# Later loads, one more addition on VectorE and later subtractions in a fused dynamic convolution and maxout layer

## The chip, the cores and the metric

The kernel runs on one core of a Trainium2 chip. The metric is the device time of one execution in microseconds (us), lower is better. Engines are named as the profile names them: PE is TensorE (PEld its weight loads), DVE is VectorE, ACT is ScalarE, POOL is GpSimd, SP is SyncE, which here only starts transfers.

## What is computed

The reference takes x (8 batches of 4160 positions with 192 channels), softmax logits weight_gen (8 heads, 7 taps per position) and three weight matrices. Cut to what matters:

```python
w = softmax(weight_gen, axis=-1)                       # 7 taps for each of 8 heads
x_pad = concatenate([zeros((B, 6, D)), x], axis=1)
out[b, s, h, g] = sum_k w[b, s, h, k] * x_pad[b, s + k, h, g]
x2 = out.reshape(33280, 192)
h1 = x2 @ w1 ; h2 = x2 @ w2                            # 192 x 1024 each
result = maximum(h1, h2) @ w_out                       # 1024 x 192
```

So each position is a weighted sum of itself and the six positions before it, followed by a two-branch layer with a maximum and an output product. The kernel uses max(h1, h2) = h1 + relu(h2 - h1): PE multiplies y by the difference w2 - w1 (the tile `wd`), ACT takes the relu, and the part y @ w1 @ w_out goes through a product `w10` of 192 x 192.

## The kernel before, in words

**Layout.** Partition p holds 260 consecutive positions of one batch element, called columns. `BATCHES` cuts the 260 columns into 16 groups of 16 and one of 4, `UNITS` cuts these into 8 units of 4 columns (batches 0 and 1 of the schedule) and after them units of 8. A unit of n columns gives n `TILES`, each a share of the 1024 hidden features for all columns of the unit. The order of the columns is rotated by 8: what the schedule calls column c of batch 0 is column c + 8 of a partition (`actual`, line 106).

**Stages of one unit.** The exponential of the logits (`exp_sum`, line 158, ACT), the sums over taps (`red`, 178, DVE), their logarithm (`ln`, 182, ACT), its subtraction from the logits (`shift`, 188, DVE), the exponential of the result as bf16 weights (`weights`, 194, ACT), the product of the weights with seven shifted views of x (`mul`, 208, and for the very first units `mul_pair`, 224, DVE), and the sum of the seven products. From batch 2 on that sum is three additions on DVE (`adds`, 234) into `y_t`, and a DMA transposes it (`transpose`, 258), behind which a small cast on POOL (`gate`, 270) waits and releases the next loads. In batches 0 and 1 PE forms sum and transpose together: `sum_part` (296) multiplies the products by an identity, tap by tap, for three of six blocks at a time, and ACT copies the result into `yt` (316). Where `adds` is called with `first=True`, DVE adds taps 3 to 5 to taps 0 to 2, and PE sums only the taps of `LEFT` = (0, 1, 2, 6). Before, this is done for unit 5.

**Hidden and output.** `hid_tile` (354) computes a tile of h2 - h1 in PSUM, `relu` (369) copies it to `rd_t` on ACT, and the output columns are accumulated in PSUM from `rd_t` (`out_hidden`, 394) and from y (`out_first`, 409), copied by ACT (`evac`, 470) and stored by SP.

**What sets the order.** Each engine executes its instructions in program order, which the kernel writes by hand. `hidden(g)` (552) emits one group of two or three tiles together with the output columns that are due, and calls back at set places: `amid` ahead of the group's last hidden tile, `between` after the copies, `beside` for the stages of later batches (ahead of the last relu where four columns go out, at the end where two do). `early` (905) lists what the first groups do there. From tile 16 on, `extra` (956) emits DVE's work for later batches at fixed tiles, `adds` takes a `beside` that puts pieces of `shift` or `red` between its additions, and ACT's exponentials and logarithms are given a due tile in `due` (929), with exceptions in `AT` and with a rule in `softmax_steps` that puts a long one off.

**Start.** SP issues the first logits, the first ten columns of x (`xs`, cast by DVE into `xb_t`), and the weight matrices; POOL issues the rest of x as casting loads, each held behind an instruction by `behind` (325). The load of schedule columns 4 to 7 of batch 0 (columns 12 to 15 of a partition) is `load_x(0, 4, 4)`. `mul_pair(0, 4, 0, 0, 4)` (line 714) multiplies taps 0 to 3 of its first two columns and needs none of it, `mul_pair(0, 4, 0, 4, K)` (719) is the first to need it. `w_diff` (686) forms the parts of `wd` on DVE, `halves_swapped` (690) swaps their halves through PE and ACT. `keep_warm` (667) runs matmuls whose result is not used. `wrap_mask` (148) zeroes, on ACT, the halo of the unit in which the rotated columns wrap around, ahead of the product for the second half of batch 15.

Of the kernel before, what the change touches and what calls it, by code (L numbers as in the profile page):

```python
# [23 lines left out]
def kernel(  # L24
# [27 lines left out]
    NB = len(BATCHES)  # L52
# [105 lines left out]
    def exp_sum(b, i=0, of=1):  # L158
        if i == 0:
            e_ts[b] = pe_.tile([P, BATCHES[b][1] * WGC], FP32, name="e_t", tag="e")  # L160
        w = BATCHES[b][1] * WGC // of
        return nc.scalar.activation(out=e_ts[b][:, i * w:(i + 1) * w], in_=wg_ts[b][:, i * w:(i + 1) * w], func=AF.Exp)  # L162
# [120 lines left out]
    LEFT = (0, 1, 2, K - 1)  # L283
# [332 lines left out]
    with tc.tile_pool(name="pstage", bufs=1) as pstage:  # L616
# [40 lines left out]
        nc.vector.tensor_single_scalar(out=msk_i, in_=msk_i, scalar=RPB - 1, op=ALU.bitwise_and)  # L657
        nc.vector.tensor_single_scalar(out=msk_i, in_=msk_i, scalar=1, op=ALU.min)
        nc.vector.tensor_copy(out=msk, in_=msk_i)
        first_exp = exp_sum(0, 0, 2)  # L660
        for step in (red, ln, shift):
            step(0, 0, 2)
        weights(0, 0)
# [13 lines left out]
        for j, parts in enumerate((((0, PAD), (PAD, 2)), ((PAD + 2, 2),))):  # L677
            for at, n in parts:
                nc.vector.tensor_copy(out=xb_ts[0][:, at * D:(at + n) * D], in_=xs[:, at * D:(at + n) * D])
            first_mul = mul_pair(0, 0, j)  # L680
            if j == 0:
                keep_warm(8, True)
        w1 = {kind: pstage.tile([P, w], BF16, name="w1" + kind)
              for kind, w in (("E", F), ("T", HF))}
# [13 lines left out]
        w1t = pstage.tile([P, F + HF], BF16, name="w1t")  # L698

        w_diff("E", 0, 0)  # L700
        behind(first_exp, load_x(0, 4, 4))
        behind(first_mul, load_x(0, 8, 4))
        load_x(0, 12, 4)
        for h in range(2):
# [8 lines left out]
            nc.sync.dma_start_transpose(out=w1t[:, c0:c0 + w].rearrange("p (b t) -> p b t", t=P), in_=w1[kind])  # L713
        mul_pair(0, 4, 0, 0, 4)
        sum_transpose(0, amid=lambda: halves_swapped(0, warm[:, 512:1024]))
        keep_warm(2)
        w_diff("T", 0, 2)
        halves_swapped(2, warm[:, 0:512])
        mul_pair(0, 4, 0, 4, K)
# [93 lines left out]
    def end_of_1():  # L813
        mul(1, 12)
        shift(2)


    def sums_in_range():
# [76 lines left out]
    none = lambda: None  # L895
    begun = {}

    def first_of_sum(u):
        begun[u] = sum_part(u, 0, 3)

    def rest_of_sum(u):
        sum_part(u, 3, 6)
        begun[u]()

    early = {
        3: (none, rest_of_1),
        4: (lambda: (behind(relu_of[8], load_x(2, 0, 8, halo=False)),
                     rest_of_sum(4), behind(yt_of[4], load_wg(4, nc.gpsimd)), ln(2)), end_of_1),
        5: (lambda: (exp_sum(3), red(3), sum_transpose(5, LEFT), weights(2, 0)), none),
        6: (lambda: (weights(2, 8), ln(3), rest_of_sum(6)), none),  # L910
        7: (lambda: (behind(relu_of[14], load_x(2, 8, 8)), rest_of_sum(7)), none),
    }
# [13 lines left out]
        ('l', 12, 0): 162,  # L926
        ('l', 5, 0): 45,
    }
    due = {}
    for c in range(3, NB):  # L930
        soon = c < 8
# [24 lines left out]
    def extra(t):  # L956

        u, k = TILES[t]
        b, o, n = UNITS[u]
        s = o + k  # L960

        if s == 0 and b + 1 < NB:
            mul(b + 1, 0)
        later = 0 if b < 4 else 5
        if s == later and b + 1 < NB:

            c = b + 1
            adds(c, 0, beside=lambda i, of: shift(c + 1, i, of) if c + 1 < NB else None)
        if s == 8 and b == NB - 3:
            wrap_mask()  # L970
        if s == 8 and b + 2 < NB:
            mul(b + 1, 8)
        if s == 8 + later and b + 2 < NB:
            adds(b + 1, 8, beside=lambda i, of: red(b + 3, i, 2) if b + 3 < NB and i < 2 else None)
        if k == n // 4 - 1 and 7 < u + 1 < NU:
            transpose(u + 1)

# [11 lines left out]
    for g in range(4, len(GROUPS)):  # L989
        if GROUPS[g][1] == 3 and "c" not in ps:  # L990
            later_ps()
        tiles = [t for t in range(GROUPS[g][0], sum(GROUPS[g])) if t >= 16]
        if g == 9:
            behind(relu_of[16], load_x(3, 0, 8))
        if g in early:
            hidden(g, OUTS[g], early[g][0],
                   amid=lambda: first_of_sum(g) if g != 5 else None)
            early[g][1]()
            steps(g, tiles)
        else:  # L1000
            hidden(g, OUTS[g], beside=lambda: steps(g, tiles))
# [35 lines left out]
```

## Time and profile before

| | us |
|---|---|
| median of 3 runs | 411.01 |
| lowest, highest | 410.79, 412.25 |
| the profiled execution | 411.17 |
| its span, first to last instruction | 409.4 |
| PE busy in it | 398.0 |
| DVE busy | 377.2 |
| ACT busy | 353.8 |

How to read the rows: a row of the timeline is start, busy time, engine, line, operation, what is written from what, shape and count; in brackets stands the idle time of the engine ahead of it and what ended that. A row of stretches has the length, then busy time and count of PE, PEld, DVE, ACT and POOL, the granted clock of PE, the share of the DMA engines and GB/s. Line numbers are those of the kernel before.

### The profile page before, as it was taken

Reading aid. Unit: us, or ns where it says so; the run is one execution under the profiler, and the core shown is the slowest. Engines: PE = TensorE matmul, PEld = TensorE weight load, DVE = VectorE, ACT = ScalarE, POOL = GpSimd, SP = SyncE. Lnnn points to the kernel's source line nnn. Section 1 sums busy time; section 2 is a strip of 40 time slices with the busy share of each in tenths; the row PEclk is TensorE's granted clock in tenths of the full one; section 3 lists DMA queues with packets and bytes.
Section 4 is the critical chain, followed back from the end, with each engine's and each line's share of the span. In section 5 each row is a group of like instructions: output and inputs, shape, how many; then the busy total and the mean of one; then the engine's idle time right before and its main releaser. Section 6 shows DMA issues by size and latency. Waiting matters only on the chain.

```text
span 409.4 us, 16186 instructions
## 1 busy us (share of the span) xinstructions
PE 398.0 (97%) x7406; PEld 317.0 (77%) x7406; DVE 377.2 (92%) x230; ACT 353.8 (86%) x418; POOL 81.2 (20%) x108
## 2 busy tenths in 40 slices
PE   8799999999999999999999999999999999999995
PEld 3588899777777877777777777877787777777795
DVE  6999999999999999999999999999999999999400
ACT  3889899999899998898988999999999889898781
POOL 1411012212221202221221122222111223120000
PEclk9999999999999999999999999999999999999998
DMA  8997298876657665776765676587478558835323
GB/s 242 250 176 208 66 194 152 170 170 164 162 114 210 188 141 117 231 200 87 230 186 109 143 217 188 107 214 187 103 120 250 145 107 228 171 79 158 98 79 120
DMA packets 65110, 66.32 MB, mean 162 GB/s; under 512 B 49425, under 2 KB 54161, under 8 KB 65040
## 3 DMA queue, kind: packets, MB, share of 16 engines
q1 hardware_dynamic: 56064, 40.54, 36.9%
q0 software_dynamic: 8832, 24.63, 29.3%
q8 instruction: 58, 0.95, 0.9%
q10 hardware_dynamic: 144, 0.10, 0.1%
q14 instruction: 12, 0.10, 0.1%
HBM read 37.33 MB, written 25.56 MB: 154 GB/s over the span
## 4 chain that ended last, share of the span: by engine, by line
PE 89%; ACT 6%; DMA 1%; issue 1%; SPq 1%; DVE 0%; ACTq 0%
PE op_ps L402 40%; PE hd L362 38%; PE op_ps L415 7%; ACT rd_t L372 3%; PE hdp L362 2%; PE yps L307 2%; DMA ws1T<-in_moe_w_dram 1%; ACT yt L316 1%; ACT e_t L162 0%; ACT o_t L487 0%; SPq L642 0%; ACT en_t L202 0%; SPq L625 0%; ACT xb_t L150 0%; SPq L634 0%
## 5 line engine op out<-in xcount | busy, mean ns | idle before, releaser
L372 ACT ACTIVATE rd_t<-hd 128x1024 bf16<-128x1024 f32 (+1 forms) x206 | 234.5, 1187 | 26.2 <-PE hd L362 25.0
L402 PE MATMUL op_ps<-wo,rd_t 64*128 64x192 bf16 x4160 | 210.6, 243 | 0.4 <-issue 0.4
L402 PEld LDWEIGHTS <-rd_t 64*128 64x128 bf16 x4160 | 180.8, 94 | 16.0 <-issue 0.6
L362 PE MATMUL hd<-yt,wd 64*128 64x512 bf16 (+1 forms) x1584 | 187.3, 360 | 0.4 <-ACT rd_t L372 0.4
L218 DVE TENSOR_TENSOR m_t<-xb_t,en_t 128x10752 bf16<-128x10752 bf16 (+1 forms) x35 | 181.5, 5191 | 0.8 <-ACT en_t L202 0.5
L362 PEld LDWEIGHTS <-wd 64*128 64x128 bf16 x1776 | 93.9, 94 | 44.8 <-issue 3.6
L270 POOL CAST gate<-yt 128x1 f32<-128x1 bf16 x29 | 42.1, 1451 | 257.8 <-DMA yt<-y_t 257.8
L244 DVE TENSOR_TENSOR m_t<-m_t 128x4608 bf16<-128x4608 bf16 (+1 forms) x30 | 74.1, 2470 | 0.1
L487 ACT COPY o_t<-op_ps 128x384 f32<-128x384 f32 (+1 forms) x99 | 57.1, 587 | 12.4 <-PE op_ps L402 12.4
L415 PE MATMUL op_ps<-w,yt 64*128 64x192 bf16 x768 | 54.7, 243 | 0.1
L415 PEld LDWEIGHTS <-yt 64*128 64x128 bf16 x768 | 37.8, 94 | 16.3 <-issue 1.1
L250 DVE TENSOR_TENSOR m_t<-m_t 128x3072 bf16<-128x3072 bf16 (+1 forms) x29 | 50.0, 1723 | 0.1
L202 ACT ACTIVATE en_t<-wg_t 128x896 bf16<-128x896 f32 (+2 forms) x45 | 35.8, 819 | 0.7 <-DVE wg_t L191 0.7
L253 DVE TENSOR_TENSOR y_t<-m_t 128x1536 bf16<-128x1536 bf16 (+1 forms) x29 | 27.3, 941 | 0.5
L133 POOL DMA_DIRECT2D xb_t<-in_x_dram x34 | 18.3, 538 | 32.9 <-ACT rd_t L372 22.0
L191 DVE TENSOR_TENSOR wg_t<-wg_t,ln_t 128x280 f32<-128x280 f32 (+5 forms) x46 | 22.1, 480 | 0.4 <-ACT ln_t L186 0.3
L372 ACT ACTIVATE rd_t<-hdp 128x1024 bf16<-128x1024 f32 x16 | 16.3, 1032 | 2.8 <-PE hdp L362 2.8
L162 ACT ACTIVATE e_t<-wg_t 128x896 f32<-128x896 f32 (+2 forms) x18 | 16.2, 903 | 1.3 <-DMA wg_t<-in_weight_gen_dram 1.3
L180 DVE TENSOR_REDUCE s_rest<-e_t 128x64 f32<-128x448 f32 (+2 forms) x27 | 16.3, 602 | 0.8 <-ACT e_t L162 0.8
L362 PE MATMUL hdp<-yt,wd 64*128 64x256 bf16 x192 | 13.9, 270 | 2.1 <-ACT rd_t L372 1.5
L477 DVE COPY o_last<-op_ps 128x192 f32<-128x192 f32 x1 | 0.4, 358 | 16.5 <-ACT o_last L477 16.5
L307 PE MATMUL yps<-ident,m_t 64*128 64x64 bf16 x636 | 12.5, 190 | 1.7 <-issue 1.1
(53 smaller groups left out, 89.8 us busy)
## 6 DMA issues: line engine op xcount, KB each, us to landing
out_dram<-o_t SPq DMA_DIRECT2D x22, 768.0 KB, 5.2
xb_t<-in_x_dram POOLq DMA_DIRECT2D x30, 384.0 KB, 5.1
out_dram<-o_t SPq DMA_DIRECT2D x20, 384.0 KB, 3.2
wg_t<-in_weight_gen_dram POOLq DMA_DIRECT2D x13, 448.0 KB, 5.3
xb_t<-xb_t POOLq DMA_DIRECT2D x15, 288.0 KB, 5.6
xb_t<-in_x_dram POOLq DMA_DIRECT2D x4, 192.0 KB, 6.7
xs<-in_x_dram SPq DMA_DIRECT2D x1, 576.0 KB, 3.8
ws0E<-in_moe_w_dram SPq DMA_DIRECT2D x2, 256.0 KB, 5.8
```

What stands on the lines that cost most here:

```text
L191: nc.vector.tensor_tensor(out=w_t, in0=w_t, in1=_sub(s_ts[b], hs.start, [[1, hs.stop - hs.start], [0, K]]), op=ALU.subtract)
L202: nc.scalar.activation(out=_sub(en_ts[b], (o * WGC + j * N * K) * 2, [[2 * N, K], [2, N], [1, 2]]), in_=_sub(wg_ts[b], (o * H + j * N) * K ...
L218: return nc.vector.tensor_tensor(out=m_out, in0=x_in, in1=_sub(en_ts[b], o * WGC * 2, [[2, K * n * H], [0, G // 2], [1, 2]]), op=ALU.mult,)
L244: nc.vector.tensor_tensor(out=taps(0, 1, 3), in0=taps(0, 1, 3), in1=taps(3, 1, 3), op=ALU.add)
L250: nc.vector.tensor_tensor(out=taps(0, 2, 2), in0=taps(0, 2, 2), in1=taps(1, 5, 2), op=ALU.add)
L253: nc.vector.tensor_tensor(out=_sub(y_ts[b], o * D, [[64, 2], [P, 3 * w // 2], [1, 64]]), in0=taps(0, 1, 1), in1=taps(2, 1, 1), op=ALU.add,)
L270: nc.gpsimd.tensor_copy(out=gate, in_=yt[:, 0:1])
L362: nc.tensor.matmul(hid_out(t, f, j), lhsT=wd_at(j, s, f // 4, f % 4 * P, P), rhs=_sub(yt_ts[u][half(j), :], (s + j) % 3 * P, [[3 * P, w // ...
L372: relu_of[t0] = nc.scalar.activation(out=rd[:, k * 1024:(k + n) * 1024], in_=hd[:, at:at + n * 1024], func=AF.Relu)
L402: return nc.tensor.matmul(op_out(c), lhsT=rd[half(r), k * 1024 + at:k * 1024 + at + P], rhs=wo[half(r), f * D:(f + 1) * D], start=start, s ...
L415: nc.tensor.matmul(op_out(c + j), lhsT=yt_ts[u][half(j), (3 * i + (s + j) % 3) * P:(3 * i + (s + j) % 3 + 1) * P], rhs=w10[half(j), s * D: ...
L487: nc.scalar.copy(out=_sub(o, c % 24 * D, [[D, len(qs)], [h * D, 2], [1, D]]), in_=_sub(tile_, at + (qs[0] - p) * D, [[D, len(qs)], [512, 2 ...
```

## The change

Four edits.

1. `load_x(0, 4, 4)` waits for the first product of DVE (`mul_pair(0, 0, 0)`) instead of the first exponential of ACT. The two matmuls of `keep_warm(2)` after the first sum are gone.
2. Unit 7 (schedule columns 28 to 31) gets the addition of taps 3 to 5 on DVE, and PE sums the four taps of `LEFT` for it.
3. In group 5 the exponential of batch 3 is emitted ahead of the last hidden tile and its relu, and no longer after the group's copies.
4. For batches 13, 14 and 15 `shift` is no longer spread in three pieces over the additions of the unit two ahead of its product, but comes in two pieces around the additions of the unit after that; the `weights` of these batches are due later (tiles 16 (c - 1) and 16 (c - 1) + 5).

```diff
-        first_exp = exp_sum(0, 0, 2)
+        exp_sum(0, 0, 2)
...
             first_mul = mul_pair(0, 0, j)
             if j == 0:
+                behind(first_mul, load_x(0, 4, 4))
                 keep_warm(8, True)
...
-        behind(first_exp, load_x(0, 4, 4))
         behind(first_mul, load_x(0, 8, 4))
         load_x(0, 12, 4)
...
         sum_transpose(0, amid=lambda: halves_swapped(0, warm[:, 512:1024]))
-        keep_warm(2)
         w_diff("T", 0, 2)
...
     def end_of_1():
         mul(1, 12)
         shift(2)
+        adds(1, 12, True)
...
+    TAPS = {7: LEFT}
+
     def first_of_sum(u):
-        begun[u] = sum_part(u, 0, 3)
+        begun[u] = sum_part(u, 0, 3, TAPS.get(u, range(K)))
 
     def rest_of_sum(u):
-        sum_part(u, 3, 6)
+        sum_part(u, 3, 6, TAPS.get(u, range(K)))
...
-        5: (lambda: (exp_sum(3), red(3), sum_transpose(5, LEFT), weights(2, 0)), none),
+        5: (lambda: (red(3), sum_transpose(5, LEFT), weights(2, 0)), none),
...
+    LATE = (13, 14, 15)
+    for c in LATE:
+        AT['W', c, 0], AT['W', c, 8] = 16 * (c - 1), 16 * (c - 1) + 5
...
-            adds(c, 0, beside=lambda i, of: shift(c + 1, i, of) if c + 1 < NB else None)
+            adds(c, 0, beside=lambda i, of: shift(c + 1, i, of) if c + 1 < NB and c + 1 not in LATE else None)
...
-            adds(b + 1, 8, beside=lambda i, of: red(b + 3, i, 2) if b + 3 < NB and i < 2 else None)
+            adds(b + 1, 8, beside=lambda i, of: (shift(b + 2, 0, 2) if i == 0 and b + 2 in LATE else None,
+                                                 red(b + 3, i, 2) if b + 3 < NB and i < 2 else None))
+            if b + 2 in LATE:
+                shift(b + 2, 1, 2)
...
-                   amid=lambda: first_of_sum(g) if g != 5 else None)
+                   amid=lambda: first_of_sum(g) if g != 5 else exp_sum(3))
```

## The prediction

> **What bounds the kernel now.** I read the page first, then the busy time by stretches, then the timeline of those stretches in which an edit lies.
>
> ```profile
> PE 398.0 (97%) x7406; PEld 317.0 (77%) x7406; DVE 377.2 (92%) x230; ACT 353.8 (86%) x418; POOL 81.2 (20%) x108
> ```
> ```profile
> 12.70:24.00 11.30, 9.03 (x241) 7.31 (x241) 11.20 (x12) 10.42 (x19) 3.23 (x6) 1.00 1.29 221
> ...
> 50.00:360.00 310.00, 309.74 (x5443) 245.31 (x5440) 309.55 (x174) 282.32 (x318) 68.10 (x81) 1.00 0.70 166
> ```
>
> The columns of the stretches are length, then busy time of PE, PEld, DVE, ACT and POOL. From 50 to 360 us PE works 309.74 of 310.00 us, so there only fewer matmuls or a new hole in PE matter. DVE works 309.55 us of them too, but ahead of PE. From 12.7 to 24 us it is DVE that never rests (11.20 of 11.30) while PE does (9.03): there DVE and, behind it, ACT set the pace. So an edit before 24 us is judged by DVE, a later one by PE.
>
> **Part 1: columns 12 to 15 of x later, two warm-up matmuls gone.**
>
> ```profile
> 4.20 0.68 POOL L133 DMA_DIRECT2D xb_t<-in_x_dram  x1 [2.79 <-ACT e_t L162]
> ...
> 6.54 1.56 DVE L227 TENSOR_TENSOR m_t<-xb_t,en_t 128x2688 bf16<-128x2688 bf16 x1
> ...
> 8.47 1.56 DVE L227 TENSOR_TENSOR m_t<-xb_t,en_t 128x2688 bf16<-128x2688 bf16 x1
> ...
> 10.34 1.06 POOL L133 DMA_DIRECT2D xb_t<-in_x_dram  x2 [5.47 <-DVE m_t L227]
> ...
> 12.12 0.69 DVE L687 TENSOR_TENSOR wd<-ws1T,ws0T 128x512 bf16<-128x512 f32 x1 [0.62 <-DMA ws1T<-in_moe_w_dram]
> ...
> 12.73 2.22 DVE L227 TENSOR_TENSOR m_t<-xb_t,en_t 128x1152 bf16<-128x1152 bf16 x2
> ...
> 14.87 0.61 DVE L180 TENSOR_REDUCE s_first<-e_t 128x64 f32<-128x448 f32 x1
> ...
> 15.59 0.25 ACT L186 ACTIVATE ln_t<-s_first 128x64 f32<-128x64 f32 x1
> ```
>
> The load now waits for the first multiplication, which ends at 6.54 + 1.56 = 8.10 us. The second ends at 8.47 + 1.56 = 10.03 and the loads behind it are issued at 10.34, so a release takes 0.31 us: the moved load is issued at about 8.4 instead of 4.20 us. On POOL's queue it stays first, and the next two loads at 10.34 find the queue free. Its first reader is the first of the two multiplications at 12.73 us (taps 4 to 6 of the pair at column 4; taps 0 to 3 need only columns cast from xs). When does it land? Next come the KB and the us from issue to landing of the moved load itself and of the one issued at 10.34, then least, median and most of all loads of x, then 11 to 12 us by the busy view.
>
> ```profile
> xb_t<-in_x_dram POOLq DMA_DIRECT2D x1, 192.0 KB, 6.8
> ```
> ```profile
> xb_t<-in_x_dram POOLq DMA_DIRECT2D x1, 192.0 KB, 6.7
> ```
> ```profile
> DMA to landing us min/median/max: 3.8/5.2/7.5
> ```
> ```profile
> 11.00:12.00 1.00, 1.00 (x44) 0.76 (x44) 0.50 (x1) 0.59 (x1) 1.00 (x3) 1.00 1.06 308
> ```
>
> The last but one column is the DMA engines' share, 1.06: no room is free while the moved load is in flight. From both sides: 8.4 + 3.8 = 12.2 and 8.4 + 7.5 = 15.9 us. The nearest rows (6.8 and 6.7) give 15.1; I take 6.2 us, thus 14.6, because the SP transfers that it shares the engines with run out earlier than before, now that it does not take turns with them from 7 to 10 us. Before, it landed at 11.0 and was needed at 12.73: 1.7 us of cover, all gone. So the multiplication starts at 14.6 instead of 12.73: DVE **+1.9 us** (-0.5 to +3.2).
>
> What waits behind it on DVE: the second multiplication, the sum at 14.87, the second half of the weights' difference, the next shift. The logarithm on ACT (15.59) waits for that sum, and behind it on ACT stand the exponential of batch 1, the second relu and everything else; PE's second sum of taps waits for the multiplications. In this stretch DVE has 0.1 us of rest, so nothing takes the delay back. What comes sooner, w_diff of ws1T (its wait of 0.62 us goes, as that transfer no longer shares with x) and the first hidden tiles, is in front of the same logarithm and gives nothing. The two warm-up matmuls ran while PE waited for that difference, so their removal is 0.
>
> The Trainium skill (DMA: Bandwidth & Descriptors, "Anatomy of one DMA") fits a DMA by a fixed 2.0 us plus bytes over 436 GB/s; for this load that is about 2.5 us (an estimate by that page), a landing before 11 us and no delay. The traces' least, 3.8 us, disagrees, so the rows stand in the sum.
>
> **Part 2: unit 7 (columns 28 to 31) with one addition on DVE, exp of batch 3 before the last relu of its group.**
>
> ```profile
> 30.88 1.36 DVE L244 TENSOR_TENSOR m_t<-m_t 128x2304 bf16<-128x2304 bf16 x1
> ...
> 38.52 1.02 ACT L372 ACTIVATE rd_t<-hdp 128x1024 bf16<-128x1024 f32 x1 [0.92 <-PE hdp L362]
> ...
> 39.80 0.96 ACT L162 ACTIVATE e_t<-wg_t 128x896 f32<-128x896 f32 x1
> ...
> 40.79 1.09 DVE L180 TENSOR_REDUCE s_rest<-e_t 128x128 f32<-128x896 f32 x1 [0.82 <-ACT e_t L162]
> ...
> 42.16 0.62 PE L307 MATMUL yps<-ident,m_t 64*128 64x64 bf16 x31 [0.33 <-issue]
> ...
> 42.39 5.76 DVE L218 TENSOR_TENSOR m_t<-xb_t,en_t 128x10752 bf16<-128x10752 bf16 x1 [0.51 <-ACT en_t L202]
> ...
> 46.74 0.79 PE L307 MATMUL yps<-ident,m_t 64*128 64x64 bf16 x42 [0.46 <-ACT yt L316]
> 47.34 0.84 PE L362 MATMUL hdp<-yt,wd 64*128 64x256 bf16 x12
> ...
> 48.22 1.02 ACT L372 ACTIVATE rd_t<-hdp 128x1024 bf16<-128x1024 f32 x1 [0.61 <-PE hdp L362]
> ...
> 49.29 1.49 PE L362 MATMUL hd<-yt,wd 64*128 64x256 bf16 x24
> ```
>
> (All times of before; part 1's delay is added to them at the end.) The addition is 1.36 us, the twin of the one at 30.88. DVE rests 0.82 + 0.51 = 1.33 us there, both rests ended by ACT work that now comes earlier: exp (0.96) fits into the 0.92 us in which ACT waits before 38.52. So the addition costs DVE nothing. On PE 4 of 7 taps remain: 36 of 84 matmuls go. Forty-two take 47.34 - 46.74 = 0.60 us to the next tile, 14 ns each, so 18 save 0.26 and both halves 0.52. The first half counts in full; of the second, PE's tile at 49.29 starts as the relu of 48.22 ends, so that relu also has to move, which it does by the first half's 0.26. The earlier exp could give up to 0.9 more, about its own length, but PE's sum at 42.16 stops in the middle for "issue", a wait that ACT does not end, so I count none of it. Together **-0.35 us** (-0.26 to -1.2).
>
> **Part 3: shifts and weights of batches 13, 14 and 15 later.** DVE's instructions change little, ACT's get a new place.
>
> ```profile
> L191 DVE TENSOR_TENSOR wg_t<-wg_t,ln_t 128x280 f32<-128x280 f32 (+5 forms) x46 | 22.1, 480 | 0.4 <-ACT ln_t L186 0.3
> ```
> ```profile
> 16.75 0.62 DVE L191 TENSOR_TENSOR wg_t<-wg_t,ln_t 128x448 f32<-128x448 f32 x1
> ```
> ```profile
> 342.41 1.60 POOL L270 CAST gate<-yt 128x1 f32<-128x1 bf16 x1 [9.21 <-DMA yt<-y_t]
> ```
> ```profile
> 343.73 1.48 PE L362 MATMUL hd<-yt,wd 64*128 64x512 bf16 x12
> ```
>
> Three subtractions of about 0.48 become two of 0.62: 0.2 us less of DVE per batch, and one unit of y comes over 1 us sooner. That is worth something only if PE waits for y. The second of the two tiles at 343.73 (344.5 us) is the first to read the transposed y whose landing POOL's gate marks at 342.41: a lead of 2 us, which DVE's delay does not eat because PE is delayed about as much. So 0. The weights:
>
> ```profile
> 348.38 1.07 ACT L202 ACTIVATE en_t<-wg_t 128x896 bf16<-128x896 f32 x1
> 349.33 1.90 ACT L372 ACTIVATE rd_t<-hd 128x2048 bf16<-128x2048 f32 x1
> 349.37 5.75 DVE L218 TENSOR_TENSOR m_t<-xb_t,en_t 128x10752 bf16<-128x10752 bf16 x1
> ...
> 357.49 1.88 ACT L372 ACTIVATE rd_t<-hd 128x2048 bf16<-128x2048 f32 x1 [0.33 <-PE hd L362]
> ...
> 359.56 1.26 ACT L150 ACTIVATE xb_t<-xb_t,msk 128x1152 bf16<-128x1152 bf16 x1 [0.19 <-issue]
> 360.72 1.00 ACT L372 ACTIVATE rd_t<-hd 128x1024 bf16<-128x1024 f32 x1
> ...
> 362.53 0.19 PEld L415 LDWEIGHTS <-yt 64*128 64x128 bf16 x5 [0.36 <-issue]
> ```
> ```profile
> 300.77 0.80 ACT L487 COPY o_t<-op_ps 128x768 f32<-128x768 f32 x1 [0.29 <-PE op_ps L402]
> ```
>
> The first half of batch 15 moves to where the row at 348.38 stands and ends at 349.45, just as DVE wants it (349.37): nothing, or 0.1 on DVE. The second half goes in front of the relu at 357.49. It takes 349.33 - 348.38 = 0.95 us of ACT, of which about 0.5 lay idle there; the mask (359.56) and the relu behind it (360.72) come 0.35 to 0.45 later, and PE, which already waits 0.36 us at 362.53 for the copy after them, waits so much longer: **+0.35 us** (0 to +0.5). Of the other four one keeps its place, and three go from before a long relu to behind one, where ACT has rested 0.29 us before the next copy at 300.77 and its like: 0.
>
> **Sum.** +1.9 - 0.35 + 0.35 = +1.9 us. The profiled execution took 411.17 us for a span of 409.4, so 1.8 us lie around the span and do not change; it stands 0.16 above the median 411.01, from which I count: **412.9 us**. A measurement here can tell about 0.5% from no change, 2.05 us: 409.0 to 413.1 is "the same".
>
> **Rivals.**
>
> *The load lands later still* (the other side: slower). If x needs 6.7 to 7.5 us from issue, as its own and the neighbouring load did, it lands at 15.1 to 15.9, DVE loses 2.4 to 3.2 and the kernel takes 413.4 to 414.2. It decides from 6.35 us of landing on. For it: DMA share 1.06; against it: SP's transfers end sooner.
>
> *The load lands early.* At 3.8 to 4.4 us from issue it lands by 12.8 and costs 0.1 at most; then parts 2 and 3 leave 410.5 to 411.2. The page's fit above leads here too. Against it: the short landings are of later, quieter stretches.
>
> *Instruction fetch and ACT give more.* If the stop at 42.16 does not recur, part 2 gives 1.2 instead of 0.35: 412.0.
>
> *PE cools.* PE's first hidden tiles, 13.92 + 1.37 = 15.3 us now, end up to 0.6 sooner, near 14.7, and its next sum waits for DVE's multiplications (now 12.73 + 2.22 = 14.95) until about 16.9: a hole of 2.2 us.
>
> ```profile
> 1.64 6.85 PE L672 MATMUL warm<-ident 128*128 128x512 bf16 x18 [1.64 <-DVE ident L655]
> ...
> 8.33 1.89 PE L672 MATMUL warm<-m_t,ident 128*128 128x512 bf16 x8
> ...
> 13.92 1.37 PE L362 MATMUL hdp<-yt,wd 64*128 64x256 bf16 x21 [0.36 <-ACT wd L694]
> ```
>
> Cold matmuls took 6.85 / 18 = 0.38 us, warm ones 1.89 / 8 = 0.24. Cold again from 17 us on, PE's work of the next 4 us would grow by 2: 415. The Trainium skill (TensorE: Matmul & The Clock Gate, Part 1) puts the drop at an idle window of about 3.4 us; by that rule it stays warm. In the rows of stretches above the clock column (the last but two) is 1.00.
>
> **How the numbers follow.** Forecast (landing 5.5 to 6.35 after issue, 412.2 to 413.1) 0.42; landing later 0.40; early (under 5.5) 0.08; fetch 0.07; cold PE 0.03. Range 410.8 to 414.2, which leaves out the cold PE and the tails of the late and early landings. Slower by over 0.5%: late and cold, 0.43; faster by over 0.5%: only if the early landing meets a gain that I don't see, 0.05; same 0.52.
>
> **What would show it.** DVE's multiplication of taps 4 to 6 at 14.6 us with an idle of about 2.5 us in front, ended by the DMA of x; w_diff of ws1T near 11.5 without its wait; the logarithm at 17.5; DVE's rests near 43 us gone; the tile now at 49.29 at about 50.8; PE's wait near 364 at 0.7. Wrong if the multiplication starts before 13.5, or if PE's tile at 50 us has no delay though DVE has.

## The result and the profile after

The changed kernel takes 414.84 us (median of 5 runs, 414.74 to 415.14) against 410.94 us (410.67 to 412.25) for the kernel before beside it: a ratio of 1.0097, 95% interval 1.0080 to 1.0113. The prediction of 412.9 us had the sign and half of the size; the time lies above its range, which ended at 414.2. The profiled execution took 414.77 us for a span of 413.0, so 1.8 us lie around the span as before, and the span is 3.6 us longer.

PE has 38 matmuls and as many weight loads fewer (busy time by engine):

```profile
PE 398.4 (96%) x7368; PEld 317.8 (77%) x7368; DVE 379.0 (92%) x228; ACT 353.9 (86%) x418; POOL 79.0 (19%) x108
```

Two stretches, the columns as in the prediction:

```profile
12.70:24.00 11.30, 7.67 (x155) 5.99 (x156) 9.42 (x10) 8.15 (x16) 2.29 (x4) 0.85 1.25 225
50.00:360.00 310.00, 309.63 (x5456) 245.54 (x5453) 309.24 (x169) 281.71 (x319) 66.98 (x82) 1.00 0.69 166
```

From 50 to 360 us nothing is new. In the first stretch DVE is down from 11.20 to 9.42 us of work, and the clock column reads 0.85 instead of 1.00. The timeline of that stretch, POOL, DVE and ACT:

```profile
8.38 0.67 POOL L133 DMA_DIRECT2D xb_t<-in_x_dram  x1 [6.97 <-DVE xb_t L679]
...
14.40 2.23 DVE L227 TENSOR_TENSOR m_t<-xb_t,en_t 128x1152 bf16<-128x1152 bf16 x2 [1.99 <-DMA xb_t<-in_x_dram]
...
17.18 0.26 ACT L186 ACTIVATE ln_t<-s_first 128x64 f32<-128x64 f32 x1 [1.88 <-DVE s_first L180]
```

The multiplication of taps 4 to 6 waits 1.99 us for the moved load and starts **1.67 us** later than before (14.40 for 12.73), as forecast (1.9). PE behind it:

```profile
16.68 0.79 PE L307 MATMUL yps<-ident,m_t 64*128 64x64 bf16 x42 [1.78 <-DVE m_t L227]
...
17.81 1.67 PE L362 MATMUL hdp<-yt,wd 64*128 64x256 bf16 x12 [0.34 <-DVE wd L688]
...
22.41 0.83 PE L362 MATMUL hdp<-yt,wd 64*128 64x256 bf16 x12 [0.92 <-ACT rd_t L372]
```

The same tiles before:

```profile
16.13 1.25 PE L362 MATMUL hdp<-yt,wd 64*128 64x256 bf16 x12 [0.23 <-DVE wd L687]
...
19.84 0.83 PE L362 MATMUL hdp<-yt,wd 64*128 64x256 bf16 x12 [1.19 <-ACT rd_t L372]
```

PE now has a hole of 1.78 us, and the twelve matmuls at 17.81 take 1.67 us; before the change the same twelve, at 16.13, took 1.25. The tile now at 22.41 stood at 19.84: +2.57, which is 1.67 and another **0.90**. Stretches cut at the borders of the clock record show why:

```profile
14.13:17.54 3.41, 1.56 (x57) 1.11 (x51) 3.14 (x4) 1.38 (x3) 0.55 (x1) 1.00 1.17 217
17.54:20.96 3.42, 3.15 (x61) 2.74 (x63) 3.32 (x6) 2.57 (x5) 0.54 (x1) 0.50 1.40 203
20.96:24.37 3.41, 2.21 (x47) 1.79 (x44) 3.23 (x3) 3.41 (x7) 0.00 (x0) 1.00 1.79 196
```

For 3.41 us, and just then, PE was granted half its clock, after a stretch of 3.41 us in which it worked 1.56. Not every execution had this: a stretch of 3.41 us at half the clock takes 0.004 off the mean granted clock of 413 us, and of the five runs of the changed kernel the one of 415.14 us has a mean of 0.999 (the profiled one 0.992). It was the longest of the five, so what the half clock adds to the time of a run doesn't follow from this one profile.

Around unit 7, PE alone:

```profile
39.97 0.40 PE L402 MATMUL op_ps<-wo,rd_t 64*128 64x192 bf16 x5 [0.64 <-issue]
44.79 0.59 PE L307 MATMUL yps<-ident,m_t 64*128 64x64 bf16 x29 [0.67 <-issue]
49.33 0.53 PE L307 MATMUL yps<-ident,m_t 64*128 64x64 bf16 x24 [0.41 <-ACT yt L316]
...
51.62 1.49 PE L362 MATMUL hd<-yt,wd 64*128 64x256 bf16 x24
```

The tile that stood at 49.29 is at 51.62: +2.33, so this stretch gives back **0.24**. The stops that the profile puts down to "issue" stay: 0.64 and 0.67 here and 0.55 at 31.96, 1.86 us in all for 1.57 before (0.52, 0.30, 0.42, 0.33).

Near the mask, ACT and PE:

```profile
360.31 1.90 ACT L372 ACTIVATE rd_t<-hd 128x2048 bf16<-128x2048 f32 x1
362.06 1.28 ACT L150 ACTIVATE xb_t<-xb_t,msk 128x1152 bf16<-128x1152 bf16 x1
363.21 1.04 ACT L372 ACTIVATE rd_t<-hd 128x1024 bf16<-128x1024 f32 x1
...
365.05 0.42 PE L415 MATMUL op_ps<-w,yt 64*128 64x192 bf16 x6 [0.23 <-ACT o_t L487]
```

The relu ahead of the mask no longer waits, the mask follows at once, and PE waits 0.23 us for ACT. Before, PE ended the work ahead at 362.48 (361.00 + 1.48) and began these matmuls at 362.53, with 0.05 us of rest: **+0.2** by the end of this stretch.

And the end. First before, then after: the last copy on DVE, and from a list of DMA queues and transfers of the time behind it the last stores (us from issue to landing) and, after the change, a fetch of instructions.

```profile
405.10 0.36 DVE L477 COPY o_last<-op_ps 128x192 f32<-128x192 f32 x1 [16.53 <-ACT o_last L477]
```
```profile
out_dram<-o_last ACTq DMA_DIRECT2D x1, 96.0 KB, 2.5
out_dram<-o_last SPq DMA_DIRECT2D x1, 96.0 KB, 2.6
```
```profile
407.62 0.36 DVE L477 COPY o_last<-op_ps 128x192 f32<-128x192 f32 x1 [18.17 <-ACT o_last L477]
```
```profile
q8 instruction: 1, 0.02, 1.6%
...
out_dram<-o_last ACTq DMA_DIRECT2D x1, 96.0 KB, 3.8
out_dram<-o_last SPq DMA_DIRECT2D x1, 96.0 KB, 3.7
```

The last copy is 2.52 us later, the end of the span 3.60: from copy to end it takes 5.37 us (413.0 - 407.62) for 4.29 before, **+1.08**. In the trace's record of transfers fifteen of the sixteen DMA engines land their share of these stores by 409.9 us and one at 411.4 and 411.7. A packet of 16 KB of instructions ran from 408.84 to 410.20, and the late share's transfers begin at 410.19. The record doesn't name the engine of a packet: that the two shared one is read from these times. Before, the last such packet began at 403.62, ahead of the last copy.

So the 3.6 us between the two profiles are 1.67 (load), 0.90 (clock), -0.24 (unit 7 with its stops), 0.2 (mask) and 1.08 (end). The prediction's sum had the first, third and fourth: 1.63 together, for the 1.9 that it forecast.

### The profile page after: what moved, and what is told of

Its sections match the earlier page's. It is cut to its first block, busy times and chain, and to the rows that moved or that the text cites. A ratio compares the mean times of both kernels' runs of the same rounds, so it can differ in the third digit from the quotient of the medians.

```text
span 413.0 us, 16108 instructions
## 1 busy us (share of the span) xinstructions
PE 398.4 (96%) x7368; PEld 317.8 (77%) x7368; DVE 379.0 (92%) x228; ACT 353.9 (86%) x418; POOL 79.0 (19%) x108
## 4 chain that ended last, share of the span: by engine, by line
PE 88%; ACT 6%; DMA 2%; DVE 2%; issue 1%; ACTq 0%
PE op_ps L402 39%; PE hd L362 37%; PE op_ps L415 7%; ACT rd_t L372 4%; PE hdp L362 2%; PE yps L307 2%; DMA xb_t<-in_x_dram 1%; DVE m_t L227 1%; DMA wg_t<-in_weight_gen_dram 1%; ACT en_t L202 1%; ACT o_t L487 0%; ACT yt L316 0%; ACT xb_t L150 0%; DVE s_first L180 0%; ACT e_t L162 0%
## 5 line engine op out<-in xcount | busy, mean ns | idle before, releaser
L270 POOL CAST gate<-yt 128x1 f32<-128x1 bf16 x29 | 40.0, 1379 | 258.9 <-DMA yt<-y_t 258.9
L244 DVE TENSOR_TENSOR m_t<-m_t 128x4608 bf16<-128x4608 bf16 (+1 forms) x31 | 75.5, 2435 | 0.2
```

Source lines behind the costliest of these rows:

```text
L244: nc.vector.tensor_tensor(out=taps(0, 1, 3), in0=taps(0, 1, 3), in1=taps(3, 1, 3), op=ALU.add)
L270: nc.gpsimd.tensor_copy(out=gate, in_=yt[:, 0:1])
```

## The experiments

The theory to test: these five terms, the end's as a matter of where the blocks of 256 PE instructions (16 KB, 128 pairs of weight load and matmul) end. The rivals: PE's longer rows are mere waits; the end is late because everything is; the stops belong to the work. The table collects what the traces of all kernels show: ratio to the kernel before run beside it; start of the multiplication of taps 4 to 6; whether a stretch between 17 and 32 us had the half clock; the sum of PE's stops for "issue" between 22 and 50 us; from the last copy to the end of the span; start of the last 16 KB packet counted from that copy.

| kernel | ratio (95%) | taps 4 to 6 | half clock | stops | copy to end | last packet |
|---|---|---|---|---|---|---|
| before | 1 | 12.73 | no | 1.57 | 4.29 | -1.5 |
| changed | 1.0097 (1.0080 to 1.0113) | 14.40 | yes | 1.86 | 5.37 | +1.2 |
| e1 load back | 1.0023 (1.0010 to 1.0036) | 12.89 | no | 2.16 | 5.07 | +1.4 |
| e2 load alone | 1.0059 (1.0037 to 1.0080) | 14.22 | no | 1.84 | 4.21 | -1.4 |
| e3 gap filled | 1.0082 (1.0059 to 1.0105) | 15.42 | no | 1.92 | 5.51 | +1.3 |
| e4 pairs restored | 1.0026 (1.0010 to 1.0042) | 16.04 | yes, twice as long | 0 | 3.98 | -1.3 |
| e5 load back, pairs | 1.0010 (0.9999 to 1.0022) | 12.45 | no | 2.40 | 4.20 | -0.9 |
| e6 before + 38 | 0.9978 (0.9958 to 0.9998) | 12.82 | no | 2.11 | 3.54 | -3.1 |
| e7 before + 90 | 1.0084 (1.0065 to 1.0102) | 12.17 | yes, at 28.6 | 4.31 | 4.94 | +1.4 |
| e8 third edit alone | 0.9999 (0.9982 to 1.0016) | 12.92 | no | 1.62 | 3.76 | -1.3 |
| e9 unit 7 alone | 1.0023 (1.0010 to 1.0037) | 12.50 | no | 1.92 | 5.18 | +1.5 |
| e10 unit 7, pairs | 1.0014 (0.9997 to 1.0030) | 12.32 | no | 4.26 | 4.20 | -1.5 |
| e11 change, gap and pairs | 1.0036 (1.0018 to 1.0055) | 14.13 | no | 2.67 | 3.70 | -1.5 |
| e12 logits later | 1.0092 (1.0071 to 1.0113) | 14.07 | no | 1.44 | 5.12 | +1.5 |
| e13 change, 38 late | 1.0101 (1.0086 to 1.0117) | 14.42 | yes | 1.61 | 3.63 | -1.4 |
| e14 unit 7, 36 late | 1.0034 (1.0022 to 1.0046) | 12.09 | no | 1.30 | 3.66 | -1.4 |
| e15 change again | 1.0090 (1.0065 to 1.0115) | 14.63 | yes, at 19.2 | 2.01 | 5.24 | +1.3 |
| e16 as e13 | 1.0071 (1.0051 to 1.0092) | 14.09 | no | 1.48 | 3.61 | -1.5 |
| e17 as e9 | 1.0025 (1.0008 to 1.0042) | 13.17 | no | 1.94 | 5.51 | +1.8 |
| e18 as e14 | 1.0010 (0.9996 to 1.0024) | 12.83 | no | 1.73 | 3.66 | -1.4 |

Runs of one kernel differ by 2 to 4 us here (the changed kernel in e15: 413.14 to 415.86; the kernel before beside e5: 410.48 to 414.63), so a single profile gives places and prices, and the ratios give the size.

**e1, the load put back** (and the first exponential kept as what releases it).

```diff
-                behind(first_mul, load_x(0, 4, 4))
...
+        behind(first_exp, load_x(0, 4, 4))
```

> The changed kernel with the load of columns 12 to 15 of x put back behind the first exponential; everything else as changed. Theory (the added time is load +1.7, PE granted half its clock +0.9, unit 7 -0.3, mask +0.2, last stores +1.1): the hole of about 2 us in PE before its second sum of taps closes, the clock record stays at 1.00 from 17 to 21 us, and the kernel is 2.5 us faster than the changed one: 412.0 to 412.6. Rival (the clock has nothing to do with the hole, or PE's longer rows at 17.8 to 20.6 us are only waits): 1.7 us faster, 413.0 to 413.3. Rival (the last stores come late because of the load's delay): about 411.2.

Measured 412.08 us, as the theory had it: the clock stays at 1.00, and of the change's 1.0097 a 1.0023 is left. The trace has the larger part of it at the end (5.07 us for 4.29) and 0.43 us ahead of it (last copy at 405.53 for 405.10).

**e2, the load alone**, the reverse edit in the kernel before.

> The kernel before with the load alone moved behind the first multiplication; PE's instructions stay as many as before. Theory: the multiplication of taps 4 to 6 starts near 14.4 us instead of 12.73, PE has the hole and the half clock, PE at 50 us is late by 2.5, and the last stores stay as quick as before (landing 2.5 us after issue), since the 16 KB fetch stays where it is relative to PE's last instructions: 413.2 to 413.8. Rival (a load that is late shifts the end's stores as well): 414.5. Rival (no loss of clock): 412.4 to 412.9.

Measured 413.49 us. The end stays as quick as before (4.21). The last copy is 2.1 us later, 1.5 of it from the load and 0.3 from the stops; the rest I can't assign. But the half clock did not come, though PE's hole is nearly the same (1.65 us for 1.78). Stretches at the clock record's borders:

```profile
13.66:17.07 3.41, 1.76 (x60) 1.39 (x58) 2.85 (x4) 1.33 (x3) 0.95 (x2) 1.00 1.17 206
17.07:20.49 3.42, 2.77 (x82) 1.86 (x75) 3.32 (x6) 3.42 (x7) 0.54 (x1) 1.00 1.41 202
```

PE worked 1.76 of 3.41 us and kept its clock; in the changed kernel 1.56, and lost it. Where the borders fall differs from run to run.

**e3, PE's hole filled.**

```diff
-        if k0 == 0:
+        if k0 == 0 and u not in yps_of:
...
+        yps_of[1] = ps["o"].tile([P, 1024], FP32, name="yps", tag="op")
+        for _ in range(7):
+            nc.tensor.matmul(yps_of[1][:, 0:512], lhsT=ident[:, 0:P], rhs=_sub(ident, 0, [[0, 512 // P], [1, P]]),
+                             start=True, stop=True, skip_group_check=True)
         features = sum_part(1, 0, 3)
```

> The changed kernel with seven more matmuls of 128x512 on the identity in PE's hole ahead of its second sum of taps (they write to the bank that this sum then starts anew). Theory (the half clock comes from the hole and costs 0.9 us): the clock stays 1.00 from 17 to 21 us, the first tile after the sum takes 1.25 instead of 1.67 us again, PE at 50 us is earlier by 0.7 to 0.9, the kernel takes 413.8 to 414.2. Rival (what is late there is ACT and DVE, the clock costs nothing): no change, 414.7 to 415.0. Rival (the clock falls at its own time whatever PE does): the clock record still shows 0.5 and the time stays.

Measured 414.80 us: by the time alone the rival's number. The timeline tells more:

```profile
15.42 2.23 DVE L227 TENSOR_TENSOR m_t<-xb_t,en_t 128x1152 bf16<-128x1152 bf16 x2 [2.68 <-DMA xb_t<-in_x_dram]
```
```profile
18.84 1.25 PE L362 MATMUL hdp<-yt,wd 64*128 64x256 bf16 x12 [0.34 <-DVE wd L688]
...
22.51 0.83 PE L362 MATMUL hdp<-yt,wd 64*128 64x256 bf16 x12 [1.16 <-ACT rd_t L372]
```

The load landed 1.0 us later than in the changed kernel's profile, and yet the tile behind is at 22.51 for 22.41. From the multiplication to that tile it takes 7.09 us, as in the kernel before (19.84 - 12.73 = 7.11), and 8.01 in the changed one. The price of the half clock is **0.9 us** at this tile in that profile; the late landing hid it in this one. In the times nothing is shown: 1.0082 against the change's 1.0097, with intervals that overlap, and where the load landed in the other five runs isn't known.

**e4, PE's count of instructions restored** in the first warm-up (`keep_warm(18)`).

```diff
-        keep_warm(18)
+        keep_warm(14)
+        for i in range(42):
+            r = i % 2
+            nc.tensor.matmul(warm[:, 512 * r:512 * r + 64], lhsT=ident[half(r), 0:P], rhs=ident[half(r), 0:64],
+                             start=True, stop=True, skip_group_check=True)
```

> The changed kernel with 38 more pairs of weight load and matmul on PE, all in its first stretch of warm-up (14 wide and 42 narrow ones instead of 18 wide), so that PE has as many instructions as the kernel before. Theory (the last stores land late because the last 16 KB fetch of instructions now falls on one of their DMA engines, and where it falls follows from the count of PE's instructions): that fetch starts 1.5 to 2 us sooner relative to the last copy, the stores land 2.5 us after issue instead of 3.8, the kernel is 0.8 to 1.2 us faster, 413.6 to 414.0, with PE at 50 us as late as in the changed kernel. Rival (the stores are late for another reason): 414.7 to 415.0.

Measured 412.05 us, a larger gain than the theory's. The profiled execution, 413.29, is one of the slower of twelve (411.10 to 413.58). In it the load lands later still and the clock is halved for two stretches:

```profile
16.04 2.23 DVE L227 TENSOR_TENSOR m_t<-xb_t,en_t 128x1152 bf16<-128x1152 bf16 x2 [3.78 <-DMA xb_t<-in_x_dram]
```
```profile
14.22:17.63 3.41, 0.59 (x11) 0.29 (x5) 1.59 (x2) 1.00 (x1) 0.55 (x1) 1.00 1.16 200
17.63:21.04 3.41, 2.72 (x60) 2.31 (x62) 3.31 (x7) 2.21 (x5) 0.54 (x1) 0.50 1.39 206
21.04:24.46 3.42, 2.88 (x60) 2.44 (x57) 3.42 (x2) 2.56 (x6) 0.00 (x0) 0.50 1.68 175
```

Yet the tile after unit 7 is at 51.18, 0.44 us sooner than in the changed kernel, since not one stop for "issue" is left, and the end takes 3.98 us instead of 5.37. So the count seems to have moved two things at once, the end and the stops. The next four runs take them apart.

**e5, e4 with the load put back; e6 and e7, the kernel before with 38 and with 90 more pairs; e8, the third edit alone.** The edits are those above with 42 and 94 narrow matmuls, and the part of the diff from `LATE` on.

> The changed kernel with the load put back and with PE's 38 pairs restored in the first warm-up (14 wide and 42 narrow matmuls). Theory (the count of instructions decides where PE stops for fetches between 24 and 50 us, 1.6 us in the kernel before, 1.9 in the changed one, none with the pairs restored, and whether the last fetch falls on the last stores): against the kernel before, unit 7 gives -0.5, the stops -1.6, the mask +0.2, the last stores 0: 409.0 to 409.5, faster than both kernels. Rival (the stops vanished in the run with restored pairs only because its load came 1.6 us later there, not by the count): 410.9 to 411.2.

> The kernel before with 38 more pairs of weight load and matmul in PE's first warm-up and nothing else. Theory (count of instructions): no idle of PE put down to issue between 24 and 45 us, where there are four of 0.30 to 0.52 us now, so 1.0 to 1.6 us faster: 409.4 to 410.0; the last fetch starts about 1.6 us sooner than now relative to the last copy and touches no store. Rival (stops belong to the work itself, wherever the blocks of instructions end): 410.9 to 411.2.

> The kernel before with 90 more pairs in PE's first warm-up, which puts the borders of 256 instructions at the end where the changed kernel has them (38 pairs fewer, a whole block of 128 pairs more). Theory: the last 16 KB fetch starts after the last copy's issue, falls on one of the DMA engines of the last stores, and the time from last copy to end grows from 4.3 to 5.2 to 5.5 us: +1.0 us from that, with some stops of PE between 24 and 50 us moved as well: 411.5 to 412.5. Rival (the last stores of the changed kernel are late for another reason): end as quick as now, 4.3 us.

> The kernel before with the third edit alone (subtractions and weights of batches 13 to 15 later); PE's instructions stay as many, in the same order. Theory: +0.2 us at the mask near 363 us, nothing anywhere else: 411.1 to 411.4. The prediction's term: +0.35. Rival (the later weights bring PE waits for y): waits of PE ended by the transposed y after 300 us and 411.6 or more.

Measured 411.83, 411.16, 415.25 and 411.21 us. e8 is right: the third edit costs 0.2 us at the mask, which no time can tell. e5 and e6 contradict the theory in one point: added pairs do not take the stops away. PE of e5 and of e7:

```profile
36.59 0.30 PE L307 MATMUL yps<-ident,m_t 64*128 64x64 bf16 x9 [1.70 <-issue]
```
```profile
27.44 0.30 PE L307 MATMUL yps<-ident,m_t 64*128 64x64 bf16 x9 [2.69 <-issue]
...
46.91 0.49 PE L362 MATMUL hdp<-yt,wd 64*128 64x256 bf16 x5 [1.39 <-issue]
```

The count deals the stops out anew: PE stands still until 2.3 to 2.6 us after a 16 KB packet began (packets at 34.18 in e5, at 24.81 and 44.50 in e7, four at 26.94 to 39.80 before), and how much of that shows depends on what PE has left to do. That the stops belong to the blocks and not to the work can be counted in the records: all 20 profiles together have 62 idle times of PE (over 0.15 us) put down to issue, and each of the 62 stands ahead of a matmul whose number is 96 more than a multiple of 128 (the 480th, 608th, 736th and 864th before), whatever tile that is. They end 2.2 to 2.9 us after the start of a packet, and once, behind a packet of 2.0 us, 3.6. e7, the kernel before with nothing but other warm-up matmuls (four wide ones fewer, 94 narrow ones more), is by its ratio 3.5 us slower, nearly as much as the changed kernel. Its end takes 4.94 us with the packet behind the last copy. In its stretches a stop alone halves the clock:

```profile
25.15:28.57 3.42, 1.13 (x35) 1.13 (x35) 2.66 (x1) 0.98 (x3) 0.00 (x0) 1.00 0.82 226
28.57:31.98 3.41, 3.41 (x32) 2.47 (x28) 2.78 (x1) 1.86 (x6) 0.00 (x0) 0.50 0.01 2
```

**e9, the second edit alone; e10, with its 36 pairs restored in the warm-up** (40 narrow matmuls and 14 wide ones).

> The kernel before with the second edit alone (unit 7 with four taps on PE and one more addition on VectorE, exponential of batch 3 ahead of the last relu); PE has 36 pairs fewer. Theory: 36 matmuls of 14 ns, -0.5 us, at the tile near 49 us beside what the stops put down to issue do (1.6 us between 24 and 45 us before, about the same here, since no pair is missing ahead of unit 7); then the last 16 KB fetch falls on the last stores and the time from last copy to end grows from 4.3 to 5.1 to 5.4 us: 411.2 to 411.9, so the edit loses what it gained. The prediction's account (-0.35, nothing at the end): 410.6.

> The second edit alone with 36 pairs restored in PE's first warm-up. Theory: end back to 3.8 to 4.3 us after the last copy; -0.5 of unit 7 kept; the stops between 24 and 50 us come out differently from the kernel before, by 0 to 2.4 us in all (none, 2.4 and 2.1 us in the three runs with 38 pairs added so far), so 409.0 to 411.4, against the second edit alone about 1 us faster. Rival (the end does not follow the count): end 5.1 us or more.

Measured 411.91 and 411.43 us. In e9 the tile after unit 7 is at 48.49 us, 0.80 sooner than before; the start was 0.23 sooner and the stops 0.35 longer, so the edit gives 0.9 us there. Worked out in the same way, the later profiles with this edit alone give 0.5 (e17, e18) and 0.2 (e14). The time of e9 is 0.9 us longer all the same, and from the last copy on it takes 5.18. In e10 the end is right (4.20) and the stops eat the gain (4.26 for 1.57).

**e11, hole filled and count restored at once** (38 matmuls of 128x96 in place of e3's seven); **e12, the logits of batch 1 held until the multiplication of taps 0 to 3.**

```diff
-        load_wg(1, nc.sync)
...
+        behind(mul_pair(0, 4, 0, 0, 4), load_wg(1, nc.sync))
```

> The changed kernel with 38 matmuls of 128x96 in PE's hole ahead of its second sum of taps: they fill the hole and restore the count at once. Theory: clock 1.00 throughout from 17 to 21 us, from the multiplication's start to PE's next hidden tile but one 7.1 us as in the runs with full clock (7.1, 7.2, 7.1) and not 8.0 as in those with half of it (8.0, 8.0), and the end 3.8 to 4.3 us after the last copy; what is left against the kernel before is the late load (1.5 to 3.3 us at VectorE): 411.0 to 413.0. Rival (clock has no price): 8.0 us again, 412 to 414.

> The changed kernel with SP's load of the logits of batch 1 (448 KB, issued at 9.5 us) held until VectorE's multiplication of taps 0 to 3 is done, near 12 us, so that it no longer runs beside the moved load of x. Theory (the 6.0 to 7.7 us from the moved load's issue to its landing are its share of full DMA engines): it lands 4 to 5 us after issue, the multiplication starts at 12.6 to 13.5 us instead of 14.4 to 16.0, the half clock does not come; the exponential of batch 1 may wait up to 1 us for its logits: 412.0 to 413.5. Rival (the load takes 6 us whatever runs beside it): multiplication at 14.2 or later, and the exponential later still: 415 or more.

e11 took 412.39 us, within the theory's range: 7.09 us from multiplication to tile, 3.70 at the end. e12 took 414.54, and neither side was right. The moved load landed 5.1 us after its issue (14.05 - 8.93) while SP's queue moved only 0.06 MB in its last 2 us; in the other kernels it took 5.5 to 6.4 and once 7.5. So 5 us of it remain when SP's transfers are held back. Nor do these explain the 7.5 of e4, where SP's queue moved nothing in the last 2 us; there POOL's queue moved 0.65 MB between the load's issue and its landing, and the load itself is 192 KB, so other transfers of its own queue ran beside it. What e12 costs is on ACT:

```profile
18.35 0.95 ACT L162 ACTIVATE e_t<-wg_t 128x896 f32<-128x896 f32 x1 [1.24 <-DMA wg_t<-in_weight_gen_dram]
```

**e13 to e18, the pairs put back where they move only the end.** In the steady stretch, ahead of one group's hidden tiles:

```diff
         rd = room(g)
+        if g == 60:
+            hd, at = hd_at[t0]
+            for i in range(38):
+                r = i % 2
+                nc.tensor.matmul(hd[:, at + 512 * r:at + 512 * r + 64], lhsT=ident[half(r), 0:P],
+                                 rhs=ident[half(r), 0:64], start=True, stop=True, skip_group_check=True)
```

> The changed kernel with 38 narrow pairs on PE in the steady stretch (ahead of the hidden tiles of group 60, into a bank that these start anew), so that everything before stays as in the changed kernel and only the borders of 256 instructions behind it move. Theory: the pairs cost 0.5 to 0.8 us of PE where they stand, the last 16 KB fetch starts 0.9 to 1.5 us ahead of the last copy instead of 1.2 us behind it, and the time from last copy to end falls from 5.4 to 3.7 to 4.3 us: 0.3 to 0.9 us faster in all than the changed kernel, with the earlier stops put down to issue as in it: 414.0 to 414.5. Rival (the end does not hang on the count, and the gain of the run with restored pairs came from its vanished stops alone): end at 5.0 or more, 415.3.

> The second edit alone with its 36 missing pairs put back in the steady stretch, ahead of the hidden tiles of group 60. Theory: PE at 50 us 0.5 to 0.9 us sooner than in the kernel before, 0.5 to 0.8 paid back for the pairs, the end 3.7 to 4.3 us after the last copy as in the kernel before: 410.5 to 411.1, and 0.3 to 0.6 faster than the second edit alone. Rival: end 5.2 us, 411.9 to 412.4.

> The changed kernel, unaltered, on the same chip as the next three, so that the pairs put back late can be judged beside it. Theory (the late last fetch costs the changed kernel 1.1 to 1.7 us at its end): 1.2 us slower at the last stores than the kernel with 38 pairs late, less the 0.5 to 0.8 that the pairs cost. Its clock and the landing of the moved load, 14.4 us in the first profile, come out again: half clock in most runs, landing 5.7 to 7.5 us after issue.

> The changed kernel with 38 narrow pairs in the steady stretch, beside the changed kernel itself. Theory: end 3.6 to 4.3 us after the last copy, 0.3 to 0.9 us faster in the median than the run before it. Rival (the end costs nothing in the median, or the pairs cost as much as they give): within 0.3 us of it.

> The second edit alone, beside the next one on the same chip. Theory: end about 5.2 us after the last copy, the fetch behind it; 0.5 to 1.0 us slower than the kernel before in the median, as in its first run (1.0023).

> The second edit alone with its 36 pairs put back late. Theory: end 3.6 to 4.3 us, 0.3 to 0.6 us faster in the median than the run before it. Rival (no gain in the median): within 0.2 us of it or slower, and then the end's gain is paid for by the pairs.

In all four with pairs late the packet is ahead of the last copy and the end takes 3.61 to 3.66 us. The stores of e16:

```profile
out_dram<-o_last ACTq DMA_DIRECT2D x1, 96.0 KB, 2.0
out_dram<-o_last SPq DMA_DIRECT2D x1, 96.0 KB, 1.9
```

In the times it shows less plainly. e13 (414.42 us) and e14 (411.67) ran beside a kernel before of 410.27 and show no gain over the first runs of the changed kernel and of e9. Side by side on one chip, the changed kernel took 414.84 and e16 413.77 us; e17 411.90 and e18 411.36: 1.07 and 0.54 us in the forecast direction, but the intervals of the ratios overlap. So the shorter end is shown in the traces, its worth in the times only made likely.

e13 and e16 are one kernel with and without the half clock: from multiplication to tile 22.44 - 14.42 = 8.02 and 21.18 - 14.09 = 7.09 us, and the profiled executions took 413.42 and 411.70. PE's first tile behind the sum in e16:

```profile
17.50 1.25 PE L362 MATMUL hdp<-yt,wd 64*128 64x256 bf16 x12 [0.34 <-DVE wd L694]
```

e15, the changed kernel again, had the half clock one stretch later, from 19.2 us, and lost 0.45 by it up to that tile (22.19 - 14.63 = 7.56). Its run with a mean clock of 0.999 took 414.57 us, the second shortest of its six.

None of the versions is shown to beat both kernels by more than a measurement can tell. e6, the kernel before with 38 pairs, has a ratio of 0.9978, but its profile (span 410.4) is longer than that of the kernel before, so what made its other runs short was not seen.

## Why the prediction was wrong

Two things that the sum put at nothing happened, the half clock (0.90 us in the profile) and the longer end (1.08). What the sum did have came to 1.63 for 1.9. The load's share is shown by taking it back and by moving it alone; the shares of the clock and of the end are prices read in the traces, and the times neither show nor deny them.

**The load (+1.9): right.** It landed 6.0 us after issue (6.2 assumed) and cost 1.67 us; the other profiles of kernels with the load behind the multiplication give 1.3 to 3.3. Its rival, a later landing, happened in e3 (6.4 us) and e4 (7.5), whose edits touch no load: by the draw of the run, as it seems; the early landing, 4.4 us or less, happened in none. Undone, it gives back most of the loss (1.0097 to 1.0023); alone it costs 1.0059.

**"PE cools" at 0.03: the step that failed first.** The prediction found the hole (2.2 us worked out, 1.78 measured), the mechanism and its place, and then set its chance at 0.03 by the idle window that the Trainium skill states. The half clock came in this profile, in e13 and e15, and for two stretches in e4. Twelve profiles at full clock have 7.09 to 7.20 us from multiplication to tile (e6, e7, e12 and e14, with other waits on that way, 7.3 to 8.4), three with the half clock over the whole way 8.01 or 8.02, so its price is 0.9 us there, and not the 2 that the rival had. The Trainium skill (TensorE: Matmul & The Clock Gate, Part 1) describes a free-running window of 3413 ns; the lengths in the clock record of these runs, 3.41, 6.83 and 10.24 us, agree. The Trainium skill also lets the clock drop after an idle window; here PE worked 1.56 of the 3.41 us ahead of the drop. That rival's 415 us is near the measured time by accident: 0.9 of clock and 1.1 at the end.

**"1.8 us lie around the span and do not change": true, but the sum ended at PE's last work, the second step that failed.** From the last copy to the end the prediction took 4.29 us as given and had no term for it, and gave no reason. It became 5.37. In all 20 profiles the order tells long ends from short ones: the last packet behind the last copy, 4.94 to 5.51 us; ahead of it, 3.54 to 4.29. The pairs of e13, e14, e16 and e18 stand far ahead of the end and leave its own instructions as they are, so there that order is what changed.

**Unit 7 (-0.35, to -1.2): about right, and hidden.** The -0.35 itself is a choice between the prediction's 0.26 and 0.52. Alone the edit gives 0.2 to 0.9 us at the tile behind (e14, e17, e18, e9); in the changed kernel the net is 0.24, just under the least that was forecast, with 0.29 more of stops. The prediction priced a removed matmul at 14 ns and nothing more. Removing it also moves the borders of all later blocks of instructions. The rival "instruction fetch gives more" let the stops only vanish; e5, e7 and e10 show them growing as well.

**The mask (+0.35): 0.2**, in e8 too. PE waits 0.23 us there in the changed kernel and 0.7 was announced; no wait for y appeared. The 0.36 us to which the prediction added stands in a row of PEld, the weight loads; PE itself rested 0.05 us there.

**Signs.** DVE waited 1.99 us for x where 2.5 were announced, w_diff of ws1T came at 11.71 for 11.5, the logarithm at 17.18 for 17.5; of DVE's two rests near 43 us one is gone and 0.27 us of the other are left. The tile came at 51.62 for 50.8: the last is the 0.9 of the clock, and the first sign against the sum.

What stays open: what starts a 16 KB packet, and at which share of work the clock falls. e10 worked 1.64 us in a stretch and kept it, e15 lost it after 1.92. The removal of the two warm-up matmuls was not tried alone. And what made the run of 415.14 us, which had no half clock, the longest of its five was not seen.

## What to carry to other kernels

A sum over the engines' work is not the time until the last store has landed: read the last copy, the last stores and the last instruction fetch as a stage of their own. Adding or taking away instructions on the engine with the most of them moves every later fetch; if an edit is worth less than 1 us, run it with the count restored as well, before its own effect is judged. And a late load may cost the clock of the engine that waits, so a hole of half a window has to be priced, with the chance that a window's border falls badly.

## What the runs showed of the hardware

- The granted clock changes only at borders 3.41 us apart, whose place against the work differs from run to run. It fell to half after stretches in which PE worked 0.59, 1.13, 1.42, 1.56 (e4, e7, e13, the changed kernel) and 1.92 us (e15) of 3.41, and stayed full after 1.64 (e10) and 1.76 (e2). The last stretches of the kernels fit in: before, it fell after 1.43 us of work (403.28 to 406.69), and in e16 it stayed after 1.52 (404.42 to 407.83). In the 20 profiles no stretch at full clock with 1.43 us of work or less was followed by another, and of those with 1.52 or more only the 1.56 and the 1.92 were not. First e15, then e10:

```profile
15.80:19.22 3.42, 1.92 (x64) 1.37 (x65) 3.32 (x7) 1.82 (x4) 1.09 (x2) 1.00 1.28 189
19.22:22.63 3.41, 2.88 (x60) 2.20 (x57) 3.41 (x3) 3.02 (x7) 0.00 (x0) 0.50 1.25 243
```
```profile
34.50:37.91 3.41, 1.64 (x66) 1.50 (x62) 3.41 (x3) 2.12 (x3) 0.54 (x1) 1.00 0.92 275
37.91:41.33 3.42, 3.42 (x112) 3.35 (x106) 2.91 (x3) 3.31 (x5) 0.54 (x1) 1.00 0.78 142
```

- Instructions come in packets of 16 KB, 58 in the changed kernel (the list of queues); by their number they are PE's, as are the stops at every 128th pair of its instructions (above):

```profile
q8 instruction: 58, 0.95, 0.9%
```

  PE's 14,736 matmuls and weight loads are 57.6 times 256. The Trainium skill (Runtime: NRT & Kernel Launch, Instruction fetch mechanics) gives blocks of that size, with which this agrees, and calls the cost of a block's border mostly hidden. From 50 us on it is, but for 0.6 us each in e6 and e7; between 22 and 50 us, where a sum of taps uses up a pair of instructions in 14 ns, it took 0 to 4.3 us of PE's time, differently for each kernel, and where a packet of 1.4 us ran just ahead of a store's last piece, the kernel's end came 1.1 later.
- The moved load, 192 KB by POOL's queue, moved its first packet 2.2 to 3.7 us after issue (11.40 for 8.38 in the changed kernel) and landed 5.1 us after issue at the least, with SP's transfers held back; the load behind it, as large, took 4.1 in the same kernel (e12).
